# A share of the exps of an attention kernel moved from ScalarE to VectorE, and extra work emitted only where it is needed

## The chip, the cores and the metric

The kernel runs on one core of a Trainium2 chip. The metric is the device time of one execution in microseconds. Times are medians of several executions. Ratios are the mean time of one kernel's fast runs over the mean time of the other's fast runs of the same rounds, so they are not quite the ratio of the medians quoted. Chips and rounds differ a little: the kernel before took 2049 us beside the changed kernel and 2042 to 2045 us beside the experiments, so kernels of different rounds are compared by ratio.

## The reference, cut to what matters

```python
B, S, D, H, Dff = 1, 2048, 512, 32, 1792
x = x + attention(layernorm(x), wqkv, wo)      # 32 heads of 16
x = x + relu(layernorm(x) @ w1) @ w2
x = x + attention(layernorm(x), wqkv, wo)      # the same weights again
x = x + relu(layernorm(x) @ w1) @ w2
```

Two attention layers of 32 heads over 2048 rows need 2 x 32 x 2048 x 2048 exps. In the trace of the kernel before, the exps keep ScalarE busy for 1847.9 us, and all matmuls, repeats included, keep TensorE busy for 1690.9 us.

## The kernel before: the parts that matter

Queries are taken 512 at a time. A block is 128 keys by 512 queries of one head. Three blocks make a slot: three score matmuls write three banks of a score buffer (there are two buffers), one exp reads all 1536 columns, and two slots later the blocks are multiplied by the values into one output bank, `ps_o`. A segment is 16 key blocks by 4 heads, 64 blocks, some 21 slots; at its end VectorE copies `ps_o` out. (A few segments of the second layer are cut into two parts by keys: what the first part summed is stored, and loaded again with the second. The change leaves these alone.) Projections and the dense layers are worked off between the slots in small pieces, through one bank, `ps_f`.

```python
while blocks:                                   # one slot
    ...
    for sg, kb, g in now:                       # what this slot needs
        run_until(("q", sg["n"]))
        run_until(("k", sg["l"], sg["T"], kb // TPC))
    ...
    for _ in range(times):                      # 1 to 3: repeats up to FLOOR = 3.4 passes a slot
        for w, (sg, kb, g) in enumerate(now):
            ...
            nc.tensor.matmul(b[:, w, :], ...)   # scores
    ex = nc.scalar.activation(out=eb[:, :m, :], in_=b[:, :m, :], func=ACTF.Exp, scale=SCALE)
    ...
    run_evac()                                  # copies out of ps_f that are due
    ...
    while len(pend) > 1:
        emit_pv()                               # the slot before last times the values
    ...
    spent = run_pe(pace) if todo else 0.0       # other matmuls, in pieces
    ...
    run_dve(900)                                # other VectorE work

def force():                                    # used by run_until
    if evac:
        run_evac()
        return True
    if cur or pick(emitted):
        cur.popleft()[1]()
        return True
    ...
```

`run_until(key)` forces work: it writes down other work at once, until the wanted result is in the lists. All this decides only the order in which each engine's instructions are written down. Every engine then works off its own list in that order and waits at an instruction until what it needs is there.

The softmax here doesn't subtract the row's maximum and nothing guards it: scores larger than these inputs give would overflow.

## Time and profile before

| | before |
|---|---|
| time, median | 2049.5 us |
| profiled span | 2037.9 us |
| exps (three blocks each) | 1366, busy 1847.9 us |
| ScalarE idle before exps | 55.1 us |
| TensorE waiting for exps | 218.8 us |
| VectorE busy | 436.9 us (21%) |
| mean granted TensorE clock | 0.971 |

Idle time ahead of the exps is time that the bound engine loses. TensorE's wait for exps is its reserve. The lines themselves stand in the prediction.

### The profile page before, as it was taken

What the parts mean: (1) busy time and instruction counts of PE and PEld (TensorE: products, weight loads), DVE (VectorE), ACT (ScalarE), POOL (GpSimd) and SP (SyncE); (2) the same over time, 40 slices, a digit from 0 to 9 for tenths busy, and PEclk for the clock granted to TensorE, in tenths of its full rate; (3) what the DMA queues carried; (4) which work ended last, traced back from release to release, by engine and by line L of the source; (5) the groups of instructions that cost most, each with busy time, mean ns of one, the idle gap of its engine ahead of it and who ended that gap; (6) DMA issues with size and microseconds to landing.
All of it is one profiled execution on the core that took longest, in us unless ns stands there. A gap on an engine that the chain in (4) does not pass through costs nothing.

```text
span 2037.9 us, 30025 instructions
## 1 busy us (share of the span) xinstructions
PE 1690.9 (83%) x13604; PEld 523.4 (26%) x13604; DVE 436.9 (21%) x927; ACT 1871.7 (92%) x1407; POOL 2.4 (0%) x35
## 2 busy tenths in 40 slices
PE   5777778888888888888889877898888888888876
PEld 2222222222222222222222222222222222222222
DVE  5111102212132132212133220211112111121122
ACT  2799999999999999999989999999999999999960
POOL 0000000000000000000000000000000000000000
PEclk8999999999999999999899989989998999989998
DMA  4000000000000000000000010000000000000000
GB/s 155 1 12 12 12 7 12 12 12 6 12 12 11 7 12 12 10 8 12 12 1 1 4 30 9 9 12 12 17 12 12 10 12 19 12 9 10 17 11 11
DMA packets 34131, 29.42 MB, mean 14 GB/s; under 512 B 17492, under 2 KB 25428, under 8 KB 34004
## 3 DMA queue, kind: packets, MB, share of 16 engines
q1 hardware_dynamic: 32420, 25.94, 5.6%
q8 instruction: 106, 1.74, 0.3%
q10 hardware_dynamic: 1584, 1.57, 0.2%
q14 instruction: 21, 0.17, 0.0%
HBM read 7.86 MB, written 2.10 MB: 5 GB/s over the span
## 4 chain that ended last, share of the span: by engine, by line
ACT 71%; PE 17%; DVE 8%; DMA 3%; issue 1%; SPq 0%; DVEq 0%
ACT e L628 71%; PE ps_s L621 6%; PE ps_f L243 5%; PE ps_o L545 4%; DMA r<-u 2%; PE ps_s L243 2%; DVE u L494 1%; DVE ht L400 1%; DVE q L371 1%; PE ps_s L579 1%; DVE stats L260 1%; DMA u<-c 1%; PE ps_f L298 0%; DVE xn L288 0%; ACT xnT L573 0%
## 5 line engine op out<-in xcount | busy, mean ns | idle before, releaser
L628 ACT ACTIVATE e<-ps_s 128x1536 bf16<-128x1536 f32 x1366 | 1847.9, 1581 | 55.1 <-PE ps_s L621 54.2
L621 PE MATMUL ps_s<-q,ktp 32*128 32x512 bf16 x7704 | 812.2, 385 | 221.2 <-ACT e L628 218.8
L545 PE MATMUL ps_o<-e,vaug 128*32 128x512 bf16 x4096 | 568.7, 396 | 45.3 <-DVE u L494 34.6
L621 PEld LDWEIGHTS <-ktp 32*128 32x128 bf16 x7704 | 257.2, 92 | 714.5 <-issue 659.7
L545 PEld LDWEIGHTS <-vaug 128*32 128x32 bf16 x4096 | 138.1, 93 | 490.3 <-issue 490.3
L243 PE MATMUL ps_f<-xn2T,w 128*128 128x512 bf16 x400 | 121.2, 391 | 11.1 <-DVE q L371 5.1
L400 DVE TENSOR_SCALAR ht<-ps_f 128x512 bf16<-128x512 f32 x99 | 68.4, 691 | 281.0 <-PE ps_f L243 281.0
L243 PE MATMUL ps_f<-w,ht 128*128 128x512 bf16 x406 | 120.0, 383 | 1.0
L499 DVE SCALAR_TENSOR_TENSOR ot<-u,mask,r 128x512 bf16<-128x512 f32 (+1 forms) x67 | 48.7, 727 | 276.5 <-DMA r<-u 273.8
L494 DVE COPY u<-ps_o 128x512 f32<-128x512 f32 x58 | 40.1, 691 | 266.5 <-PE ps_o L545 266.5
L243 PE MATMUL ps_f<-xnT,wqkv 128*128 128x512 bf16 x248 | 74.1, 389 | 1.4 <-DVE vaug L363 0.2
L371 DVE TENSOR_SCALAR q<-ps_f,mask 128x512 bf16<-128x512 f32 x68 | 47.9, 746 | 90.2 <-PE ps_f L243 90.2
L243 PE MATMUL ps_f<-wo,ot 128*128 128x512 bf16 x224 | 66.2, 386 | 0.8
L414 DVE TENSOR_TENSOR x<-x,ps_f 128x512 bf16<-128x512 bf16 x29 | 20.0, 688 | 189.2 <-PE ps_f L243 189.2
L386 DVE TENSOR_TENSOR x<-x,ps_f 128x512 bf16<-128x512 bf16 x28 | 19.2, 687 | 161.1 <-PE ps_f L243 161.1
L243 PEld LDWEIGHTS <-w 128*128 128x128 bf16 x448 | 32.0, 99 | 76.4 <-issue 67.5
L260 DVE BATCH_NORM_STATS2 stats<-x 128x6 f32<-128x512 bf16 x64 | 44.0, 687 | 7.0 <-DMA x<-in_A_x_dram 5.6
L338 DVE CAST ktp<-ps_f 128x512 bf16<-128x512 f32 x28 | 19.4, 692 | 117.1 <-PE ps_f L243 117.1
L243 PEld LDWEIGHTS <-ht 128*128 128x128 bf16 x448 | 29.1, 97 | 57.5 <-issue 47.9
L398 ACT ACTIVATE ht<-ps_s 128x512 bf16<-128x512 f32 x6 | 3.6, 597 | 42.8 <-PE ps_s L243 42.8
L298 PE MATMUL ps_f<-ident,xn 128*128 128x128 bf16 x188 | 21.8, 249 | 16.3 <-DVE xn L288 10.0
L298 PEld LDWEIGHTS <-xn 128*128 128x128 bf16 x256 | 18.4, 109 | 54.6 <-DVE xn L288 31.7
(54 smaller groups left out, 303.1 us busy)
## 6 DMA issues: line engine op xcount, KB each, us to landing
r<-u SPq DMA_DIRECT2D x63, 256.0 KB
w<-in_B_w_dram SPq DMA_DIRECT2D x2, 1792.0 KB
x<-in_A_x_dram SPq DMA_DIRECT2D x16, 128.0 KB
out_dram<-x SPq DMA_DIRECT2D x16, 128.0 KB
wqkv<-in_A_wqkv_dram ACTq DMA_DIRECT2D x3, 512.0 KB
c<-u SPq DMA_DIRECT2D x63, 8.0 KB
u<-c SPq DMA_DIRECT2D x63, 8.0 KB
wo<-in_A_wo_dram SPq DMA_DIRECT2D x1, 512.0 KB
```

The costliest lines, as they stand in the source:

```text
L243: nc.tensor.matmul(b, lhsT, rhs, start=(i == 0), stop=(i == n - 1))
L260: nc.vector.bn_stats(out=st[:], in_=x_t[j * TPC + i][:])
L298: nc.tensor.transpose(pt[:, c * P : (c + 1) * P], xnbuf[i][:, c * P : (c + 1) * P], ident[:])
L371: nc.vector.tensor_scalar(out=qbuf[n % 2][e][:], in0=b, scalar1=mask[e][:, 0:1], scalar2=None, op0=ALU.mult,)
L400: nc.vector.tensor_scalar(out=ht[ft][:], in0=b, scalar1=0.0, scalar2=None, op0=ALU.max)
L414: nc.vector.tensor_add(out=x_t[tt][:], in0=x_t[tt][:], in1=b)
L494: nc.vector.tensor_copy(out=u[:], in_=ps_o[:])
L499: nc.vector.scalar_tensor_tensor(out=ot[t][:, a : a + w], in0=u[:, a : a + w], scalar=mask[e][:, 0:1], in1=r[:, a : a + w], op0=ALU.mult, ...
L545: nc.tensor.matmul(ps_o[32 * g : 32 * g + 32, :], vaug[sg["l"]][kb][:, 4 * sg["T"] + g, 2 * e : 2 * e + 32], s["e"][:, w, :], start=(kb == ...
L579: nc.tensor.matmul(b, lhsT, rhs, start=(i == 0), stop=(i == len(mms) - 1))
L621: nc.tensor.matmul(b[:, w, :], kt[32 * g : 32 * g + 32, kc : kc + P], qbuf[sg["n"] % 2][sg["e"]][32 * g : 32 * g + 32, :], start=True, sto ...
L628: ex = nc.scalar.activation(out=eb[:, :m, :], in_=b[:, :m, :], func=ACTF.Exp, scale=SCALE)
```

## The change

The intent: VectorE is idle for four fifths of the span, so it takes up to six blocks of a segment off ScalarE, in three pairs. A score, scaled so that one unit of log2 is 2^23, is turned into an integer, whose bits are the exponent and the mantissa of the exp; a quartic in the mantissa mends the value. A pair costs VectorE two first steps out of PSUM and five more steps over both blocks. Its result comes as a sum, so TensorE multiplies it by the values three times. The first step is declared free of ScalarE's read of the same buffer (it reads another bank). `run_until` now makes only what the wanted thing depends on.

```diff
+    PAIRS = ((0, 2), (6, 8), (12, 14))
+    BACKLOG = 5000.0
 ...
+    def finish_group():
+        while cur:
+            cur.popleft()[1]()
+        run_evac()
     def run_until(key):
-        while key not in made:
-            assert force(), key
+        if key in made:
+            return
+        finish_group()
+        if key in made:
+            return
+        t = maker[key]
+        for k in (*t["deps"], *t.get("after", ())):
+            run_until(k)
+        ...
 ...
+    def flush_pair():
+        run_until(pairs[0]["key"])
+        emit_pair()
+
+    def dve_block(half, sg, kb, g, src, ex, recent):
+        while half == 0 and pairs:
+            flush_pair()
+        first = nc.vector.tensor_scalar(
+            out=di[:, half, :].bitcast(I32), in0=src, scalar1=EXP_BIAS, scalar2=0.0,
+            op0=ALU.add, op1=ALU.max,
+        )
+        tc.declare_no_dep(
+            first.ins, ex.ins, reason="both only read the scores, and in different banks"
+        )
+        ...
+            steps = (
+                (690, lambda: bits(dm, 0x007FFFFF, 0x3E800000)),
+                (1260, lambda: step(dy, dm, C2, dm)),
+                (1260, lambda: step(dy, dy, C1, dm)),
+                (1260, lambda: step(de, dy, C0, di)),
+                (690, lambda: bits(di, 0x7F800000, KAPPA_BITS)),
+            )
+    def emit_pair():
+        ...
+        for rhs in (de, de, None):
+            for half, (kb, g) in halves:
+                pv(...)
 ...
+            if half == 0:
+                taken = load[0] + sum(t["cost"] for t in dve_q) < BACKLOG
+            if not taken:
+                half = None
+        m = len(now) - (half is not None)
 ...
-        run_dve(900)
+        run_dve(500.0)
```

There is one `di`, one `dm`, one `dy` and one `de`. So the next pair cannot begin before the one before has been multiplied: `dve_block` flushes it first, and the end of a segment does the same (cut above). This is called a forced end; a pair is open until it has been multiplied. `load` is the code's own model of VectorE's work in hand, in ns, and a pair is taken only while that and the queued tasks are under `BACKLOG`.

More of the change, by code (lines that the diff above doesn't have):

```diff
@@ L1 @@
+import math
 from contextlib import ExitStack
@@ L55 @@
     NACC = 6
+    LEAD, C2, C1, C0 = 0.43216083424908747, -0.036015386827967774, 0.769178243088122, 0.36146642138144963
+    KAPPA_BITS = 0x00170000
+    LOG2E = 1.4426950408889634
+    UNIT = float(1 << 23)
+    EXP_BIAS = (126.0 + math.log2(2.0 * LEAD)) * UNIT
+    PAIRS = ((0, 2), (6, 8), (12, 14))
     FLOOR = 3.4
+    BACKLOG = 5000.0
     ctx.enter_context(tc.manual_schedule())
@@ L66 @@
     mask = [sb([P, 1], FP32, f"mask{e}") for e in range(2)]
+    qmask = [sb([P, 1], FP32, f"qmask{e}") for e in range(2)]
     wqkv = sb([P, NDC, 3 * D], BF16, "wqkv")
@@ L89 @@
     ot = [sb([P, QS], BF16, f"ot{t}") for t in range(NT)]
-    acc = [sb([P, QS], FP32, f"acc{t}") for t in range(NACC)]
+    dm = sb([P, 2, QS], FP32, "dm")
+    dy = sb([P, 2, QS], FP32, "dy")
+    di = sb([P, 2, QS], FP32, "di")
+    de = sb([P, 2, QS], BF16, "de")
+    acc = [x[:, k, :] for x in (dm, dy, di) for k in range(2)]
     ebuf = [sb([P, W, QS], BF16, f"e{n}") for n in range(NE)]
@@ L148, in mark @@
         made[key] = slot[0] + lag
-    def emitted(deps):
-        return all(k in made for k in deps)
-    def ready(deps):
-        return all(k in made and (wide[0] or made[k] < slot[0]) for k in deps)
     cur = deque()
@@ L160, with task, group, ready @@
     dve_q = []
+    maker = {}
+    load = [0.0]
+    owed = [0.0]
+    def task(cost, fn, makes=(), deps=(), after=(), first=False):
+        t = {"cost": cost, "fn": fn, "makes": makes, "deps": deps, "after": after}
+        if first:
+            dve_q.insert(first - 1, t)
+        else:
+            dve_q.append(t)
+        maker.update({k: t for k in makes})
+    def group(pieces, makes, deps):
+        g = {"pieces": pieces, "makes": makes, "deps": deps}
+        maker.update({k: g for k in makes})
+        return g
+    def ready(t):
+        return all(k in made and (wide[0] or made[k] < slot[0]) for k in t["deps"]) and all(
+            k in made for k in t.get("after", ())
+        )
     def left():
@@ L165, in left, with start_group @@
         )
-    def pick(test):
-        for q in (urgent, work):
-            for g in q:
-                if test(g["deps"]):
-                    q.remove(g)
-                    cur.extend(g["pieces"])
-                    return True
-        return False
-    owed = [0.0]
+    def start_group(g):
+        (urgent if g in urgent else work).remove(g)
+        cur.extend(g["pieces"])
     def run_pe(budget):
@@ L182, in run_pe @@
             if not cur:
-                if evac or not pick(ready):
+                g = None if evac else next((g for q in (urgent, work) for g in q if ready(g)), None)
+                if g is None:
                     break
+                start_group(g)
             c, fn = cur.popleft()
@@ L189, in run_pe, with do_task, run_dve, mm_group @@
         return spent
-    def run_dve(budget):
-        i = 0
-        while i < len(dve_q) and budget > 0:
-            c, deps, fn = dve_q[i]
-            if ready(deps):
-                dve_q.pop(i)
-                fn()
-                budget -= c
-            else:
-                i += 1
+    def do_task(t):
+        dve_q.remove(t)
+        t["fn"]()
+        load[0] += t["cost"]
+        for k in t["makes"]:
+            if k not in made:
+                mark(k)
+    def run_dve(limit):
+        while load[0] < limit:
+            t = next((t for t in dve_q if ready(t)), None)
+            if t is None:
+                return
+            do_task(t)
     def run_evac():
         while evac:
-            evac.popleft()()
-    def force():
-        if evac:
-            run_evac()
-            return True
-        if cur or pick(emitted):
-            cur.popleft()[1]()
-            return True
-        for i, (c, deps, fn) in enumerate(dve_q):
-            if emitted(deps):
-                dve_q.pop(i)
-                fn()
-                return True
-        return False
-    def run_until(key):
-        while key not in made:
-            assert force(), key
-    def run_all():
-        while force():
-            pass
-        assert not (urgent or work or dve_q or cur)
-    def mm_group(mms, fin, deps, per=2):
+            c, fn = evac.popleft()
+            fn()
+            load[0] += c
+    def finish_group():
+        while cur:
+            cur.popleft()[1]()
+        run_evac()
+    def run_until(key):
+        if key in made:
+            return
+        finish_group()
+        if key in made:
+            return
+        t = maker[key]
+        for k in (*t["deps"], *t.get("after", ())):
+            run_until(k)
+        if "pieces" in t:
+            start_group(t)
+            finish_group()
+        else:
+            do_task(t)
+        assert key in made, key
+    def run_all():
+        while True:
+            finish_group()
+            g = next((g for q in (urgent, work) for g in q if ready(g)), None)
+            if g is not None:
+                start_group(g)
+            elif dve_q:
+                do_task(next(t for t in dve_q if ready(t)))
+            else:
+                break
+        assert not (urgent or work)
+    def mm_group(mms, fin, makes, deps, per=2, cost=690):
         hold = {}
@@ L244, in piece @@
                 if a + per >= n:
-                    evac.append(lambda: fin(b))
+                    evac.append((cost, lambda: fin(b)))
             pieces.append((min(per, n - a), piece))
-        return {"pieces": pieces, "deps": deps}
+        return group(pieces, makes, deps)
     ln_seq = []
@@ L308, in ln_rows @@
         prev = ln_seq[ln_seq.index(tag) - 1]
-        dve_q.append((750, [], lambda: ln_stats(tag, j, i)))
+        task(750, lambda: ln_stats(tag, j, i), [("st", tag, i)])
         if i == TPC - 1:
-            dve_q.append((2400, [], lambda: ln_rstd(tag)))
+            task(2400, lambda: ln_rstd(tag), [("rs", tag)], after=all4("st", tag))
             for k in range(TPC):
-                dve_q.append((420, [("xT", prev, k)], lambda k=k: ln_apply(tag, j, k)))
+                task(
+                    420, lambda k=k: ln_apply(tag, j, k), [("xn", tag, k)],
+                    [("xT", prev, k)], [("rs", tag)],
+                )
     def ln_groups(tag, dst, war):
@@ L324, in fin @@
                     mark(("xnT", tag, i))
-                evac.append(fin)
-            groups.append({"pieces": [(1.3, piece)], "deps": [("xn", tag, i)] + war})
+                evac.append((430, fin))
+            groups.append(
+                group([(1.3, piece)], [("xT", tag, i), ("xnT", tag, i)], [("xn", tag, i)] + war)
+            )
         return groups
@@ L341, in k_group @@
     def k_group(l, T, j):
-        return mm_group(k_mms(T, j), lambda b: k_fin(l, T, j, b), all4("xnT", ("ln1", l, j)))
+        return mm_group(
+            k_mms(T, j), lambda b: k_fin(l, T, j, b), [("k", l, T, j)],
+            all4("xnT", ("ln1", l, j)),
+        )
     def v_mms(kb):
@@ L364, in fin @@
             mark(("v", l, kb))
-        return mm_group(v_mms(kb), fin, all4("xnT", ("ln1", l, kb // TPC)))
+        return mm_group(v_mms(kb), fin, [("v", l, kb)], all4("xnT", ("ln1", l, kb // TPC)))
     def q_group(run, n, l, j, T):
@@ L371, in fin @@
                 nc.vector.tensor_scalar(
-                    out=qbuf[n % 2][e][:], in0=b, scalar1=mask[e][:, 0:1], scalar2=None,
+                    out=qbuf[n % 2][e][:], in0=b, scalar1=qmask[e][:, 0:1], scalar2=None,
                     op0=ALU.mult,
@@ L378, in q_group @@
             [(wqkv[:, c, T * P : (T + 1) * P], xnT[j][:, c, :]) for c in range(NDC)],
-            fin, all4("xnT", ("ln1", l, j)),
+            fin, [("q", n)], all4("xnT", ("ln1", l, j)), cost=1400,
         )
@@ L391, in o_group @@
             [(ot[t][:, i * P : (i + 1) * P], wo[:, t // 2, :]) for t in range(NT)], fin,
+            [("o", l, j, i)],
             [("ot", l, j, t, i) for t in range(NT)],
@@ L406, in h_group @@
             [(w1[:, c, ft * P : (ft + 1) * P], xn2T[:, c, :]) for c in range(NDC)], fin,
-            all4("xnT", ("ln2", l, j)) + war,
+            [("h", l, j, ft)], all4("xnT", ("ln2", l, j)) + war,
         )
@@ L422, in z_group @@
             [(ht[ft][:, i * P : (i + 1) * P], w2[:, ft, :]) for ft in range(NF)], fin,
+            [("z", l, j, i)],
             [("h", l, j, ft) for ft in range(NF)],
@@ L460, in add_run @@
                     "l": l, "j": j, "t": 2 * T + e, "e": e, "T": T, "kbs": kbs, "n": n,
-                    "load": load, "store": store,
+                    "load": load, "store": store, "begun": set(),
                 }
@@ L483, in finish_segment @@
         l, j, t, e = sg["l"], sg["j"], sg["t"], sg["e"]
+        load[0] += 690
         if sg["store"]:
-            nc.vector.tensor_copy(out=acc[t][:], in_=ps_o[:])
+            nc.vector.tensor_copy(out=acc[t], in_=ps_o[:])
             return
@@ L488, in finish_segment @@
         norm_no[0] += 1
+        if n > 1:
+            run_until(("m", n - 2))
         u, r, c = ubuf[n % 2], rbuf[n % 2], cbuf[n % 2]
@@ L491, in finish_segment @@
         if sg["load"]:
-            nc.vector.tensor_add(out=u[:], in0=acc[t][:], in1=ps_o[:])
+            nc.vector.tensor_add(out=u[:], in0=acc[t], in1=ps_o[:])
         else:
@@ L526, in recip @@
                 mark(("r", n), 4)
-            dve_q.append((250, [("c", n)], recip))
-            dve_q.append((700, [("r", n)] + war, lambda: mul(0, QS)))
+            task(250, recip, [("r", n)], [("c", n)])
+            task(
+                700, lambda: mul(0, QS), [("ot", l, j, t, i) for i in range(TPC)] + [("m", n)],
+                [("r", n)] + war,
+            )
         if t == NT - 1:
@@ L533, with pv @@
     pend = deque()
-    last_exp = [None] * NE
+    exps = [deque(maxlen=6) for _ in range(NE)]
+    def pv(sg, kb, g, rhs, stop=False):
+        e = sg["e"]
+        nc.tensor.matmul(
+            ps_o[32 * g : 32 * g + 32, :],
+            vaug[sg["l"]][kb][:, 4 * sg["T"] + g, 2 * e : 2 * e + 32],
+            rhs, start=g not in sg["begun"], stop=stop,
+            tile_position=(0, 32 * g), skip_group_check=True,
+        )
+        sg["begun"].add(g)
     def emit_pv():
@@ L543, in emit_pv @@
             sg, kb, g, w = s["blocks"].popleft()
-            e = sg["e"]
-            nc.tensor.matmul(
-                ps_o[32 * g : 32 * g + 32, :],
-                vaug[sg["l"]][kb][:, 4 * sg["T"] + g, 2 * e : 2 * e + 32],
-                s["e"][:, w, :],
-                start=(kb == sg["kbs"][0]), stop=(kb == sg["kbs"][-1]),
-                tile_position=(0, 32 * g), skip_group_check=True,
-            )
-            if kb == sg["kbs"][-1] and g == 3:
+            last = kb == sg["kbs"][-1]
+            if last:
+                while pairs and pairs[0]["sg"] is sg:
+                    flush_pair()
+            pv(sg, kb, g, s["e"][:, w, :], last)
+            if last and g == 3:
                 finish_segment(sg, sg is segs[-1])
@@ L555, in emit_pv, with bits, step @@
             pend.popleft()
+    pairs = deque()
+    pair_no = [0]
+    def flush_pair():
[3 more added lines that the diff above has]
+        while half == 0 and pairs:
+            flush_pair()
+        first = nc.vector.tensor_scalar(
+            out=di[:, half, :].bitcast(I32), in0=src, scalar1=EXP_BIAS, scalar2=0.0,
+            op0=ALU.add, op1=ALU.max,
+        )
+        tc.declare_no_dep(
+            first.ins, ex.ins, reason="both only read the scores, and in different banks"
+        )
+        for earlier in recent:
+            tc.declare_no_dep(
+                first.ins, earlier,
+                reason="the scores read here were written after it, and are waited for",
+            )
+        load[0] += 690
+        if half == 0:
+            pair_no[0] += 1
+            pairs.append({"sg": sg, "key": ("e", pair_no[0]), "blocks": []})
+        pairs[-1]["blocks"].append((kb, g))
+        if half == 1:
+            def bits(out, keep, put):
+                nc.vector.tensor_scalar(
+                    out=out[:].bitcast(I32), in0=di[:].bitcast(I32), scalar1=keep,
+                    scalar2=put, op0=ALU.bitwise_and, op1=ALU.bitwise_or,
+                )
+            def step(out, x, c, y):
+                nc.vector.scalar_tensor_tensor(
+                    out=out[:], in0=x[:], scalar=c, in1=y[:], op0=ALU.add, op1=ALU.mult
+                )
+            key = pairs[-1]["key"]
+            steps = (
[4 more added lines that the diff above has]
+                (690, lambda: bits(di, 0x7F800000, KAPPA_BITS)),
+            )
+            for n, (cost, fn) in enumerate(steps):
+                k = key + (n,) if n + 1 < len(steps) else key
+                task(cost, fn, [k], after=[key + (n - 1,)] if n else [], first=n + 1)
+    def emit_pair():
+        p = pairs.popleft()
+        halves = list(enumerate(p["blocks"]))
+        tops = di[:].bitcast(BF16)
+        for rhs in (de, de, None):
+            for half, (kb, g) in halves:
+                pv(p["sg"], kb, g, tops[:, half, 1::2] if rhs is None else rhs[:, half, :])
     for j in range(NQS):
@@ L568 @@
                     op=ALU.add, axis=mybir.AxisListType.XY,
+                )
+            for e in range(2):
+                nc.vector.tensor_scalar(
+                    out=qmask[e][:], in0=mask[e][:], scalar1=SCALE * LOG2E * UNIT, scalar2=None,
+                    op0=ALU.mult,
                 )
@@ L599 @@
     level = 0.0
+    taken = False
+    recents = [[], []]
     while blocks:
@@ L626 @@
                 )
-        m = len(now)
-        ex = nc.scalar.activation(out=eb[:, :m, :], in_=b[:, :m, :], func=ACTF.Exp, scale=SCALE)
-        if last_exp[no % NE] is not None:
+        sg, kb, g = now[-1]
+        r = (kb * 4 + g - 2) // W
+        half = None
+        if len(now) == W and now[0][0] is sg and not (sg["load"] or sg["store"]):
+            half = next((p.index(r) for p in PAIRS if r in p), None)
+            if half == 0:
+                taken = load[0] + sum(t["cost"] for t in dve_q) < BACKLOG
+            if not taken:
+                half = None
+        m = len(now) - (half is not None)
+        ex = nc.scalar.activation(
+            out=eb[:, :m, :], in_=b[:, :m, :], func=ACTF.Exp,
+            scale=1.0 / (LOG2E * UNIT),
+        )
+        for earlier in exps[no % NE]:
             tc.declare_no_dep(
-                ex.ins, last_exp[no % NE],
+                ex.ins, earlier,
                 reason="the matmuls that read the buffer between the two writes order them",
             )
-        last_exp[no % NE] = ex.ins
+        exps[no % NE].append(ex.ins)
+        recent = recents[no % 2]
+        recents[no % 2] = [ex.ins] + recent[:1]
+        load[0] = max(load[0] - 50.0 - 427.0 * m, 0.0)
         run_evac()
+        if half is not None:
+            dve_block(half, sg, kb, g, b[:, W - 1, :], ex, recent)
         for sg, kb, g in now:
@@ L639 @@
             emit_pv()
-        pend.append({"e": eb, "blocks": deque(x + (w,) for w, x in enumerate(now))})
+        if pairs and ready({"deps": [pairs[0]["key"]]}):
+            emit_pair()
+        pend.append({"e": eb, "blocks": deque(x + (w,) for w, x in enumerate(now[:m]))})
         rest = len(blocks) / W % per_chunk
@@ L644 @@
         spent = run_pe(pace) if todo else 0.0
+        sg = now[-1][0]
         level = min(level + times + 1 + spent - FLOOR, 0.4)
-        run_dve(900)
+        run_dve(500.0)
     while pend:
```

## The prediction

> **What bounds the kernel now.** I read the page from the top: busy shares, the chain that ended last, then the costliest groups, and after that the timeline of a quiet stretch and the waits by engine.
>
> ```profile
> PE 1690.9 (83%) x13604; PEld 523.4 (26%) x13604; DVE 436.9 (21%) x927; ACT 1871.7 (92%) x1407; POOL 2.4 (0%) x35
> ...
> ACT 71%; PE 17%; DVE 8%; DMA 3%; issue 1%; SPq 0%; DVEq 0%
> ACT e L628 71%; PE ps_s L621 6%; PE ps_f L243 5%; PE ps_o L545 4%; DMA r<-u 2%; PE ps_s L243 2%; DVE u L494 1%; DVE ht L400 1%; DVE q L371 1%; PE ps_s L579 1%; DVE stats L260 1%; DMA u<-c 1%; PE ps_f L298 0%; DVE xn L288 0%; ACT xnT L573 0%
> ...
> L628 ACT ACTIVATE e<-ps_s 128x1536 bf16<-128x1536 f32 x1366 | 1847.9, 1581 | 55.1 <-PE ps_s L621 54.2
> ```
>
> The reader is to see that ScalarE is busy 92% of the span, that the exps are 71% of the chain, and that the exp line is busy 1847.9 us with only 55.1 us of idle before it. The mean of 1581 ns counts overlap between neighbours; 1847.9 / 1366 = 1.353 us is what one exp of three blocks (1536 columns) costs the engine. The exps run from 67 us to 1970 us, a main stretch of some 1903 us; the roughly 67 us ahead of it and 68 us behind it are not touched by the change.
>
> The next question is how much room TensorE has, because the change gives it work too. One quiet stretch, start and duration first:
>
> ```profile
> 429.55 0.83 PE L621 MATMUL ps_s<-q,ktp 32*128 32x512 bf16 x9 [0.62 <-ACT e L628]
> ...
> 430.31 0.40 PE L545 MATMUL ps_o<-e,vaug 128*32 128x512 bf16 x3
> ...
> 430.63 0.61 PE L243 MATMUL ps_f<-w,ht 128*128 128x512 bf16 x2
> ...
> 431.17 0.39 PE L621 MATMUL ps_s<-q,ktp 32*128 32x512 bf16 x3
> ...
> 431.49 0.40 PE L545 MATMUL ps_o<-e,vaug 128*32 128x512 bf16 x3
> ...
> 431.82 0.60 PE L243 MATMUL ps_f<-w,ht 128*128 128x512 bf16 x2
> ...
> 432.36 0.39 PE L621 MATMUL ps_s<-q,ktp 32*128 32x512 bf16 x3
> ...
> 433.58 0.82 PE L621 MATMUL ps_s<-q,ktp 32*128 32x512 bf16 x9 [0.50 <-ACT e L628]
> ```
>
> Starts matter here, not durations. Three score matmuls occupy 0.32 us (431.17 to 431.49), nine 0.76 us (429.55 to 430.31), so each further pass of three costs (0.76 - 0.32) / 2 = 0.22 us and a change of kind some 0.1 us. The nine are one useful pass and two repeats, which the code's floor of 3.4 passes a slot (a slot is one exp) asks for. From 429.55 to 433.58 three slots pass, 1.343 us each, and TensorE stands still only about 0.5 to 0.6 us in them. Over the whole run the waits say the same:
>
> ```profile
> PE ps_s L621 <- ACT e L628: 218.8, 604, 0.8
> ...
> ACT e L628 <- PE ps_s L621: 54.2, 109, 2.4
> ...
> PE ps_o L545 <- DVE u L494: 34.6, 39, 2.3
> ```
>
> TensorE waits for ScalarE 218.8 us in all. That is its whole reserve: whatever shortens the exps and whatever is added to TensorE both come out of it. VectorE is free for four fifths of the span.
>
> **What the Trainium skill says.** "ScalarE: Activation LUTs", section What ACT_TABLE_LOAD costs: an ACTIVATE takes 186 ns + 0.833 ns a column, and neighbours overlap by about 93 ns. For 1536 columns that is 1.37 us; the trace has 1.35. So taking 512 columns off an exp should save 0.427 us, by 0.833 x 512. No run here yet shows an exp of 1024 columns.
> "VectorE: DVE Perf Modes", section on the perf-mode tier table: fp32 single-source operations within SBUF run at twice the rate, two-source ones and anything from PSUM in fp32 at one element a cycle. The trace agrees as far as it goes: copying 512 fp32 columns out of PSUM takes 691 ns, and the two-source scalar_tensor_tensor of 512 fp32 columns 751 ns.
> "PSUM — Partial Sum Buffer", Specifications: ScalarE and VectorE may read PSUM in parallel at full bandwidth as long as they are in different banks. The change relies on it (VectorE takes the third bank of a score buffer, ScalarE the first two). The trace of before has no such case.
> "TensorEngine Tiling (Array Packing)", Key Properties: different tiles run in parallel, and changing the tiling mode drains the engine. The 0.22 us for three matmuls and the 0.1 us at a change of kind agree with both.
>
> **The change part by part.** Off ScalarE: in each of 58 segments that are neither stored nor loaded (64 blocks, 21.3 slots) up to six slots, in three pairs, give their last block to VectorE. One pair saves 2 x 0.427 = 0.854 us of exps. All 58 x 3 = 174 pairs would save 148.6 us, 7.3%.
>
> On VectorE, one pair costs: two first steps out of PSUM at 0.69 (the 691 ns row) = 1.38; two bit operations over 1024 elements at double rate, 0.69 each (512 cycles' worth, like the row of 512) = 1.38; three scalar_tensor_tensor of 1024, which I put at 751 ns plus 512 further elements at 1/0.96 ns (533), less a little for immediate scalars, 1.26 each = 3.78. Together 6.54 us. 174 pairs would be 1138 us on top of 437, so over three quarters of the span; the five steps in a row behind the second first step are 5.16 us and, with small gaps, 5.5 us.
>
> How many pairs are taken? The code refuses a pair when its modelled load plus the queued tasks exceed 5000 ns. The pairs sit at slots 0 and 2, 6 and 8, 12 and 14. After slot 2 the model issues about one step a slot, and none in a slot with an evacuation (690). At slot 6, without an evacuation in between, load 1260 plus two steps left 1950 plus reciprocal and scaling of the segment before 950 make 4160: taken. With one evacuation, one step more is left: 5420, refused. Evacuations: from the rows of the groups some 279 in 1366 slots, 0.20 a slot, so no evacuation in three slots has a chance of 0.8^3 = 0.51; layer-norm tasks (4080 at once) refuse a few more, so the second pair is taken in about 0.43 of the segments. The first I put at 0.93. The third is taken in 0.9 of the cases where the second was refused and 0.45 where it was taken: 0.57 x 0.9 + 0.43 x 0.45 = 0.70. Sum 2.06 a segment, 120 pairs. They save 120 x 0.854 = 102 us on ScalarE and bring VectorE 120 x 6.54 = 785 us, to some 1220 us.
>
> On TensorE, a moved block is multiplied by the values three times instead of once. The two blocks of a pair are two column groups apart and run side by side, in the same mode as the matmuls before: three passes of 0.22 = 0.65 us a pair, 78 us in all. The repeats of the scores are not reduced by it, since the floor doesn't count these matmuls.
>
> Lost again: where a pair follows a taken one at four slots' distance (0.43 + 0.19 = 0.62 a segment, 36 in all), the rest of the chain is forced right behind the scores. From the end of the exp two slots before the pair's second slot: the chain ends after 0.35 + 0.75 + 5.5 = 6.6 us; the scores of slot 6 are done after 1.35 + 0.93 + 2 x 1.35 + 0.32 = 5.3 us. TensorE waits 1.3 us, then 0.65 us of pair, 0.65 us of other work, 0.35 us of scores: the next exp can start at 8.2 us, whereas ScalarE is through at 7.2. So 1.0 us of ScalarE idle, 36 us in all; such a pair gains nothing. Evacuations that queue behind a step of up to 1.26 us: about half of the 279 fall into slots with a chain, 0.3 us of TensorE lost each (42 us), of which I let a third reach the exps, 14 us. Forcing work only by need can take away some of the 54.2 us; 41 of those waits, 21.3 us, lie between 1000 and 1250 us, where stored and loaded segments force work. I take 8 us.
>
> Sum for ScalarE: -102 + 36 + 14 - 8 = -60 us. TensorE has to agree: of its reserve of 218.8 go 78 for the new matmuls, 36 x 1.3 = 47 for forced pairs and 42 for late evacuations, which leaves 52 us by which the span can shrink before TensorE is full. The two limits are close, so both engines would set the end together; I choose the tighter one and predict 2049.5 - 52 = 1998 us. That VectorE's first step doesn't wait for the exp of the same scores is already in this: I let it start as soon as the scores are there.
>
> **The rivals.** First: nearly all is hidden. If VectorE keeps up and most pairs are taken, 150 pairs save 128 us, the span goes to 1920 to 1950 us. For it: VectorE is idle 79% now and double buffering swallows nearly an exp. Against it: the chain of 5.5 us against four slots of 5 us, and TensorE, which would need 128 + 98 = 226 us of a reserve of 218.8.
> Second: TensorE becomes the bound. Its idle time goes to nothing, waits of ScalarE for scores grow from 54 us to 100 us or more, and the time stays at 2005 to 2035 us. For it: the reserve above. Against it: part of TensorE's work is repeats.
> Third: the new waits on VectorE (pair matmuls, score banks released late, evacuations late) cost more than the exps save, and a TensorE that stands still is granted a lower clock: the mean is 0.971 now. Then 2050 to 2090 us. For it: after a stall of 2.39 us at 1797 us the next six exps came 1.6 to 1.9 us apart instead of 1.35. Against it: the refusal rule keeps VectorE's queue short.
>
> **Range and chances.** The middle is 1998 us (2.5% less). The range 1950 to 2037 us covers most of the first and all of the second rival. The line of 2% is 2008.5 us, near the middle; faster by over 2% 0.63, within 2% 0.31, slower by over 2% 0.06.
>
> **What would show it.** Right: the exps' busy time falls to about 1745 us, some 240 of them with 1024 columns at about 0.93 us; VectorE busy around 1220 us, its two-source steps 1.26 us each; 480 more matmuls into the output bank (three for each of the 240 moved blocks instead of one); ScalarE's waits for scores rise to about 90 to 100 us, with new waits of TensorE on the pair's last bit step. Wrong: more than 150 or fewer than 90 pairs; the reserve of TensorE (its waits on exps) still over 120 us, which would mean that I overrated its work; steps at other durations; a mean granted clock away from 0.97.

## The result, and the profile after

The changed kernel takes 2104.95 us (2100.59 to 2106.41, 4 runs) against 2049.45 us: ratio 1.0268, 95% interval 1.0248 to 1.0287. It is slower by 2.7%, where 2.5% faster was predicted, and lies outside the range.

First the page's busy line, the chain that ended last by engine, and the exp line of the changed kernel (L772 is its exp, L756 its score matmul).

```profile
PE 1758.3 (84%) x13926; PEld 542.3 (26%) x14087; DVE 1155.7 (55%) x1734; ACT 1792.3 (85%) x1407; POOL 2.4 (0%) x35
...
ACT 52%; PE 32%; DVE 13%; issue 2%; DMA 1%; another core or an unknown queue 0%; SPq 0%; DVEq 0%; ACTq 0%
...
L772 ACT ACTIVATE e<-ps_s 128x1536 bf16<-128x1536 f32 (+1 forms) x1366 | 1768.4, 1410 | 199.2 <-PE ps_s L756 195.7
```

The exps did become cheaper: busy 1768.4 us instead of 1847.9, 79.5 us less. But ScalarE's idle time before them went from 55.1 to 199.2 us, 144.1 us more. The sum, +64.6 us, is the growth of the profiled span (2101.8 - 2037.9 = 63.9 us). ScalarE's share of the chain falls from 71% to 52%; TensorE and VectorE now stand in it with 32% and 13%.

Next the groups by form (count, busy time, mean ns of one).

```profile
L772 ACT ACTIVATE e<-ps_s 128x1536 bf16<-128x1536 f32 x1135 | 1563.3, 1482 | 162.6 <-PE ps_s L756 159.3
...
L635 DVE TENSOR_SCALAR di<-ps_s 128x512 int32<-128x512 f32 x230 | 158.8, 690 | 342.3 <-PE ps_s L756 306.1
...
L661 DVE SCALAR_TENSOR_TENSOR dy<-dm 128x1024 f32<-128x1024 f32 x115 | 140.7, 1224 | 3.2
...
L772 ACT ACTIVATE e<-ps_s 128x1024 bf16<-128x1024 f32 x230 | 243.5, 1059 | 36.6 <-PE ps_s L756 36.4
...
L655 DVE TENSOR_SCALAR di<-di 128x1024 int32<-128x1024 int32 x115 | 79.6, 692 | 3.3
```

115 pairs were taken (230 first steps), and the steps cost what had been worked out: 690, 1224 and 692 ns. The cost of the work is not where the prediction failed. The waits are (engine and line, whom it waited for, us in total, times, longest):

```profile
ACT e L772 <- PE ps_s L756: 195.7, 191, 6.3
PE ps_s L756 <- ACT e L772: 132.3, 393, 0.6
...
PE ps_o L598 <- DVE de L661: 51.2, 28, 3.9
```

Before, ScalarE's longest wait for scores was 2.4 us; now it is 6.3 us. TensorE still waits 132.3 us for exps, so it is not full. New is its wait for a step of the pair, 28 times, up to 3.9 us. The longest stall in order of time (start, duration; L423 copies a query projection out of `ps_f`, L598 multiplies by the values, L287 are the other matmuls):

```profile
681.67 0.39 PE L756 MATMUL ps_s<-q,ktp 32*128 32x512 bf16 x3
681.99 0.61 PE L287 MATMUL ps_f<-xnT,wqkv 128*128 128x512 bf16 x2
682.64 1.41 DVE L423 TENSOR_SCALAR q<-ps_f,qmask 128x512 bf16<-128x512 f32 x2 [1.54 <-PE ps_f L287]
683.96 1.22 DVE L661 SCALAR_TENSOR_TENSOR dy<-dy,dm 128x1024 f32<-128x1024 f32 x1
685.21 1.23 DVE L661 SCALAR_TENSOR_TENSOR de<-dy,di 128x1024 bf16<-128x1024 f32 x1
686.47 0.69 DVE L655 TENSOR_SCALAR di<-di 128x1024 int32<-128x1024 int32 x1
686.49 1.04 PE L598 MATMUL ps_o<-de,vaug 128*32 128x512 bf16 x4 [3.89 <-DVE de L661]
...
688.29 1.03 PE L287 MATMUL ps_f<-xn2T,w 128*128 128x512 bf16 x2
689.26 0.61 PE L756 MATMUL ps_s<-q,ktp 32*128 32x512 bf16 x3
...
689.91 1.45 ACT L772 ACTIVATE e<-ps_s 128x1536 bf16<-128x1536 f32 x1 [6.34 <-PE ps_s L756]
```

Read it downward. The slot's scores come at 681.67; then the current group of projection matmuls is finished (681.99) and VectorE has to copy it out, 1.41 us, and only then come the three steps of the open pair that were left, two of which the first pair matmuls need. TensorE stands for 3.89 us with the pair's matmuls at the head of its list. This is `flush_pair`: `run_until` calls `finish_group` before the wanted steps. VectorE was idle for 1.54 us just before, waiting for that group. After the wait TensorE is slow besides: two matmuls take 1.03 us that took 0.61 us at 681.99. Two stretches of 14 us (start and end, length, busy time of PE, PEld, DVE, ACT and POOL, then the granted clock, the DMA share and GB/s):

```profile
682.00:696.00 14.00, 9.32 (x42) 1.91 (x39) 7.13 (x9) 4.88 (x5) 0.00 (x0) 0.63 0.01 2
520.00:534.00 14.00, 11.77 (x116) 3.80 (x117) 9.18 (x12) 14.00 (x12) 0.00 (x0) 1.00 0.09 19
```

Around the stall the granted clock was 0.63, and ScalarE was busy 4.88 us of 14; in a stretch with a pair that was not forced it was 1.00, and ScalarE was busy throughout.

I put every stall of the exps down to the longest wait of TensorE between 1.5 us before the stall and its end (waits for exps left out). 35 stalls with 108 us follow a wait for a pair's steps; before the change all stalls together were some 55 us. The stall shown is the worst kind and not the only one: in 18 of the 35, matmuls of a group stand between the slot's scores and the pair's matmuls (70.0 us, 3.9 us a stall); in 17 none do (38.1 us, 2.2 us a stall). The theory, called F below: the forced ends of pairs cost the time. Rivals: T, TensorE is too full with added matmuls and repeats, and S, the new way of giving out work costs time of itself.

### The profile page after: what moved, and what is told of

The parts are those of the page before. It is cut to its first block, busy times and chain, and to the rows that moved or that the text cites. A ratio compares the mean times of both kernels' runs of the same rounds, so it can differ in the third digit from the quotient of the medians.

```text
span 2101.8 us, 31777 instructions
## 1 busy us (share of the span) xinstructions
PE 1758.3 (84%) x13926; PEld 542.3 (26%) x14087; DVE 1155.7 (55%) x1734; ACT 1792.3 (85%) x1407; POOL 2.4 (0%) x35
## 4 chain that ended last, share of the span: by engine, by line
ACT 52%; PE 32%; DVE 13%; issue 2%; DMA 1%; another core or an unknown queue 0%; SPq 0%; DVEq 0%; ACTq 0%
ACT e L772 51%; PE ps_s L756 11%; PE ps_f L287 9%; PE ps_o L598 9%; DVE de L661 2%; DVE dy L661 2%; DVE ht L453 2%; DVE u L551 1%; PE ps_s L287 1%; DVE q L423 1%; DVE di L655 1%; PE ps_s L712 1%; DVE ktp L387 1%; DVE vaug L415 1%; DVE x L467 0%
## 5 line engine op out<-in xcount | busy, mean ns | idle before, releaser
L772 ACT ACTIVATE e<-ps_s 128x1536 bf16<-128x1536 f32 (+1 forms) x1366 | 1768.4, 1410 | 199.2 <-PE ps_s L756 195.7
L756 PE MATMUL ps_s<-q,ktp 32*128 32x512 bf16 x7727 | 819.8, 388 | 145.2 <-ACT e L772 132.3
L598 PE MATMUL ps_o<-e,vaug 128*32 128x512 bf16 x3866 | 586.9, 399 | 42.9 <-DVE u L551 33.7
L756 PEld LDWEIGHTS <-ktp 32*128 32x128 bf16 x7727 | 241.9, 92 | 643.2 <-issue 574.9
L635 DVE TENSOR_SCALAR di<-ps_s 128x512 int32<-128x512 f32 x230 | 158.8, 690 | 342.3 <-PE ps_s L756 306.1
L598 PEld LDWEIGHTS <-vaug 128*32 128x32 bf16 x4556 | 168.6, 94 | 599.8 <-issue 579.5
L661 DVE SCALAR_TENSOR_TENSOR dy<-dm 128x1024 f32<-128x1024 f32 x115 | 140.7, 1224 | 3.2
L661 DVE SCALAR_TENSOR_TENSOR dy<-dy,dm 128x1024 f32<-128x1024 f32 x115 | 140.7, 1223 | 3.2
L661 DVE SCALAR_TENSOR_TENSOR de<-dy,di 128x1024 bf16<-128x1024 f32 x115 | 140.7, 1223 | 3.0
L598 PE MATMUL ps_o<-de,vaug 128*32 128x512 bf16 x460 | 81.1, 403 | 51.4 <-DVE de L661 51.2
L287 PE MATMUL ps_f<-xn2T,w 128*128 128x512 bf16 x358 | 111.7, 390 | 12.4 <-issue 3.3
L287 PE MATMUL ps_f<-w,ht 128*128 128x512 bf16 x361 | 107.6, 383 | 10.0 <-issue 5.6
L655 DVE TENSOR_SCALAR di<-di 128x1024 int32<-128x1024 int32 x115 | 79.6, 692 | 3.3
L655 DVE TENSOR_SCALAR dm<-di 128x1024 int32<-128x1024 int32 x115 | 79.5, 691 | 2.9
L287 PE MATMUL ps_f<-xnT,wqkv 128*128 128x512 bf16 x209 | 68.5, 402 | 8.5 <-issue 4.6
L423 DVE TENSOR_SCALAR q<-ps_f,qmask 128x512 bf16<-128x512 f32 x68 | 47.9, 746 | 37.7 <-PE ps_f L287 35.7
L287 PE MATMUL ps_f<-wo,ot 128*128 128x512 bf16 x196 | 59.8, 383 | 5.8 <-issue 2.9
L598 PE MATMUL ps_o<-di,vaug 128*32 128x512 bf16 x230 | 55.3, 415 | 7.6 <-DVE di L655 5.2
```

The source lines that it names most:

```text
L287: nc.tensor.matmul(b, lhsT, rhs, start=(i == 0), stop=(i == n - 1))
L423: nc.vector.tensor_scalar(out=qbuf[n % 2][e][:], in0=b, scalar1=qmask[e][:, 0:1], scalar2=None, op0=ALU.mult,)
L598: nc.tensor.matmul(ps_o[32 * g : 32 * g + 32, :], vaug[sg["l"]][kb][:, 4 * sg["T"] + g, 2 * e : 2 * e + 32], rhs, start=g not in sg["begun ...
L635: first = nc.vector.tensor_scalar(out=di[:, half, :].bitcast(I32), in0=src, scalar1=EXP_BIAS, scalar2=0.0, op0=ALU.add, op1=ALU.max,)
L655: nc.vector.tensor_scalar(out=out[:].bitcast(I32), in0=di[:].bitcast(I32), scalar1=keep, scalar2=put, op0=ALU.bitwise_and, op1=ALU.bitwise_or,
L661: nc.vector.scalar_tensor_tensor(out=out[:], in0=x[:], scalar=c, in1=y[:], op0=ALU.add, op1=ALU.mult)
```

## The experiments

**No pairs.** The list of pairs is emptied; the new giving out of work stays.

```diff
-    PAIRS = ((0, 2), (6, 8), (12, 14))
+    PAIRS = ()
```

> The list of pairs is empty: no block goes to VectorE, everything else of the change stays (work forced by need, load model, shared buffers). Theory F (the loss of 55 us is the forced ends of pairs): about the time of before, 2035 to 2055 us, exps waiting some 50 us for scores. Rival S (the new way of giving out work costs time by itself): 2080 us or more, waits of the exps well over 100 us without any pair. Rival T (TensorE is full because of the added matmuls): also as before.

Measured 2035.98 us beside 2045.45 us, ratio 0.9958 (0.9920 to 0.9996), exps waiting 46.3 us for scores. S falls: this part of the change costs nothing and gains about 9 us (1 to 16 us by the interval).

**No forced end from the next pair.** A pair is refused while the one before is open.

```diff
-                taken = load[0] + sum(t["cost"] for t in dve_q) < BACKLOG
+                taken = load[0] + sum(t["cost"] for t in dve_q) < BACKLOG and not pairs
```

> A pair is refused while the pair before it is unfinished, so no pair's end is forced by the next one. Theory F: the stalls over 1 us that follow a wait of TensorE for a pair's steps (34 of them, about 108 us in the changed kernel) go, pairs fall from 115 to about 95 or so, time 1985 to 2020 us. Rival T (TensorE full, or VectorE in the way of evacuations): the stalls move elsewhere, time 2060 us or more.

Measured 1995.71 us beside 2045.45 us, ratio 0.9761 (0.9733 to 0.9788), with 97 pairs. One condition turns 2.7% slower into 2.4% faster. The waits of this kernel:

```profile
ACT e L772 <- PE ps_s L756: 78.8, 125, 5.0
...
PE ps_s L756 <- ACT e L772: 139.3, 421, 0.7
...
PE ps_o L598 <- DVE de L661: 5.9, 3, 2.6
```

TensorE's waits for `de` went from 28 to 3 (with those for the pair's last step, from 35 to 6), and the waits of the exps from 195.7 to 78.8 us. They did not move elsewhere. F holds here; as the pairs also became fewer, the next run keeps more of them.

**Two pairs, nine slots apart.** Forcing is made rarer by distance, at nearly the same number of pairs.

```diff
-    PAIRS = ((0, 2), (6, 8), (12, 14))
+    PAIRS = ((0, 2), (11, 13))
```

> Two pairs a segment, nine slots apart instead of four (three pairs before). Theory F: about 105 to 112 pairs, nearly as many as now, hardly any of them forced, exps busy about 1770 us, waits of the exps 60 to 110 us, time 1980 to 2015 us. Rival T: TensorE gets nearly the same added work (about 108 pairs), so the time stays at 2070 us or more.

Measured 2015.00 us (2013.71 to 2021.94), ratio 0.9868 (0.9834 to 0.9902), with 108 pairs, exps busy 1772.9 us and waiting 104.1 us for scores. That is the upper edge of what F allowed and far from T. Distance doesn't end forcing: seven stalls with 15.5 us still follow a wait for a pair's steps. It is slower than the run before with more pairs. TensorE waits up to 3.8 us for the copy at a segment's end here (39.0 us in all), where it was 0.8 us (31.1 us). I take it that the later pair's chain runs into that end; no run tests this.

**One multiplication instead of three.** The result is wrong (relative error 0.073).

```diff
-        for rhs in (de, de, None):
+        for rhs in (None,):
```

> A moved block is multiplied once instead of three times (the result is wrong on purpose); the pairs, the steps and the forcing stay. Theory F: TensorE's added matmuls are not the cause: 10 to 30 us less than the changed kernel, still over 2065 us. Rival T: the added matmuls are the cause, 75 us less or more, under 2030 us.

Measured 2149.95 us, ratio 1.0515 (1.0458 to 1.0572), at a mean granted clock of 0.919: slower than the changed kernel, with less work. Neither theory had expected that. 34 stalls with 111 us follow a wait for a pair's step, about as before; the other stalls grew from 91 to 129 us. It is against T, but it needed the run below.

**The same without forcing.**

```diff
-                taken = load[0] + sum(t["cost"] for t in dve_q) < BACKLOG
+                taken = load[0] + sum(t["cost"] for t in dve_q) < BACKLOG and not pairs
 ...
-        for rhs in (de, de, None):
+        for rhs in (None,):
```

> A moved block multiplied once (wrong result on purpose) and no pair forced. It tells why one_pass became slower, 45 us over the changed kernel, with less work. If the lack of matmuls alone lowers the granted clock: mean clock under 0.96 and a time over 2005 us. If it takes the forced stalls to lower it: clock about 0.98 and 1970 to 2000 us, not over no_force.

Measured 1989.56 us, ratio 0.9759 (0.9721 to 0.9796), clock 0.980 (result wrong). The ratio is that of no_force, 0.9761. So the two added multiplications cost nothing that these runs show (the intervals are 0.3 to 0.4% wide to either side) where the next pair forces nothing: T falls. Fewer matmuls alone didn't lower the clock; together with the forced stalls they did. Why the two together do so is not settled here.

**The forced end kept, but the pair's steps alone.** The pairs and their places are those of the changed kernel; the current group is no longer put in front.

```diff
     def flush_pair():
-        run_until(pairs[0]["key"])
+        key = pairs[0]["key"]
+        while key not in made:
+            do_task(dve_q[0])
         emit_pair()
```

> The changed kernel with the forced end kept (same pairs, same places) but only the pair's open VectorE steps are forced: TensorE's current group and its evacuation are no longer finished in front of them. If the loss per forced pair (3.2 us in the trace, where I had worked out 1.0) comes from the group and evacuation put in front: stalls of about 1.0 to 1.5 us each, time 2020 to 2050 us. If it comes from the chain of steps itself: 2085 us or more.

Measured 2025.84 us (2024.61 to 2026.19), ratio 0.9917 (0.9899 to 0.9935), with 114 pairs. From 1.0268 this is 3.5%, some 72 us, by the order of a few instructions. 23 stalls with 34.1 us are left behind a pair's step, 1.5 us each, none with a group in front, where it was 35 with 108 us, 3.1 us each. So about two thirds of the forced loss went with the group and its copy in front of the steps. It is what the whole edit is worth: it shifts later slots too, stalls that had no group in front among them, and 7530 score matmuls remain of 7727 (by the floor runs below I estimate these at some 4 us). At the place shown above, this kernel does this:

```profile
683.16 0.61 PE L598 MATMUL ps_o<-de,vaug 128*32 128x512 bf16 x4 [1.59 <-DVE de L663]
...
684.68 1.46 PE L758 MATMUL ps_s<-q,ktp 32*128 32x512 bf16 x9
...
686.19 1.45 ACT L774 ACTIVATE e<-ps_s 128x1536 bf16<-128x1536 f32 x1 [3.14 <-PE ps_s L758]
```

A wait of 1.59 us still becomes a stall of 3.14 us here, in part because nine score matmuls (two of the three passes are repeats) then take 1.46 us instead of 0.82.

**VectorE waits for the exp of the same scores.** no_force with the declaration taken out.

```diff
-        tc.declare_no_dep(
-            first.ins, ex.ins, reason="both only read the scores, and in different banks"
-        )
```

> As no_force (pair refused while one is open), but VectorE's first step waits for ScalarE's read of the same scores, as it would without the declaration of the change. If that wait matters: the first step comes after the exp, some 1 us later, the score buffer is released 0.7 us after the exp and the exps wait for scores at the 194 moved blocks; 20 to 80 us more than no_force, 2015 to 2075 us. If it is hidden by double buffering: 1995 to 2005 us.

Measured 2076.08 us (2063.20 to 2078.71), ratio 1.0147 (1.0105 to 1.0188), against 0.9761 for no_force: some 79 us. The waits of this kernel:

```profile
DVE di L635 <- ACT e L769: 524.1, 194, 10.4
...
ACT e L769 <- PE ps_s L753: 139.7, 227, 5.0
```

Each of the 194 first steps now waits for an exp, and VectorE's list stands behind it; TensorE in its turn waits 47.4 us for the first steps to free a score buffer. So that part of the change was needed, and double buffering does not hide it.

**No forced end, and the steps alone at a segment's end.** Both edits above together.

> no_force with the forcing that is left at segment ends (three stalls after a wait for a step, 12.0 us in no_force's trace) done by steps alone. Theory: 5 to 12 us less than no_force, 1983 to 1991 us.

Measured 1982.42 us (1982.06 to 1991.29) beside 2042.54 us, ratio 0.9716 (0.9690 to 0.9742), results correct. It is the fastest version measured, 2.8% faster than the kernel before; its interval just overlaps that of no_force, so what the second edit adds is less sure.

**Fewer repeats.** no_force with a floor of 2.8 instead of 3.4.

```diff
-    FLOOR = 3.4
+    FLOOR = 2.8
```

> no_force with a floor of 2.8 passes a slot instead of 3.4, so fewer repeats of the score matmuls. If TensorE's fullness holds the rest of the gain back: 10 us less or more than no_force, under 1986 us. If the repeats keep its clock up (as the one_pass run suggests, slower at a granted clock of 0.919): a lower granted clock and a longer time, over 2000 us.

Measured 2003.14 us (1989.84 to 2014.86), ratio 0.9805 (0.9752 to 0.9858), clock 0.938, at 5978 recorded score matmuls instead of 7650. The clock fell as the second view said; the time scatters too much to say more than that it is no gain.

**More repeats.** The best version with a floor of 3.8.

```diff
-    FLOOR = 3.4
+    FLOOR = 3.8
```

> no_force_steps_first with a floor of 3.8 passes a slot instead of 3.4: more repeats of the scores. If the clock is still what small stalls come from: clock above 0.982 and up to 10 us less. If TensorE is full enough by now: 10 to 60 us more, 1992 to 2045 us.

Measured 1998.56 us (1996.25 to 1999.04), ratio 0.9785 (0.9761 to 0.9809), clock 0.985. So more repeats cost 14 us or so: TensorE is not the bound, but its reserve is not free either.

**Pairs further apart and a longer backlog, twice.** The best version with

```diff
-    PAIRS = ((0, 2), (6, 8), (12, 14))
-    BACKLOG = 5000.0
+    PAIRS = ((0, 2), (7, 9), (13, 15))
+    BACKLOG = 7000.0
```

> no_force_steps_first with the pairs five slots apart instead of four ((0,2), (7,9), (13,15)) and a backlog limit of 7000 instead of 5000, so that the pair before is more often finished in time: 110 to 135 pairs instead of 97. Theory: each further pair is worth about 0.6 us (no_pairs to no_force_steps_first: some 54 us by 97 pairs), so 10 to 25 us less, 1958 to 1975 us. Rival (VectorE delays evacuations and the copy at the segment's end): 1980 us or more.

Measured 1994.75 us, ratio 0.9767 (0.9739 to 0.9796), with 89 pairs, not the 110 to 135 expected. My edit was careless: its second gap is still four slots, not five as I wrote. With (14, 16) as the third pair:

```diff
-    PAIRS = ((0, 2), (7, 9), (13, 15))
+    PAIRS = ((0, 2), (7, 9), (14, 16))
```

> As spaced_backlog with the third pair one slot later, so that both gaps are five slots: in spaced_backlog the second gap was still four, and only 89 pairs were taken. If the gap is what refuses pairs: 105 to 140 pairs, time 1965 to 1985 us. If late evacuations and copies eat the further pairs: more pairs, but 1985 us or more.

Measured 2006.91 us, ratio 0.9818 (0.9787 to 0.9848), with 86 pairs. Both outcomes expected were wrong: the gap is not what keeps the count down. Six waits for a pair's step, 9.9 us, are back. The traces show where the pairs went: counting the short exps by their slot, first pairs of a segment fell from 43 in no_force_steps_first to 32 and 29, second pairs rose from 15 to 26 and 29, third pairs fell from 39 to 31 and 28. A replay of the kernel's Python with the chip's calls left out, which gives the same counts, shows the reason of each refusal: in these two runs an open pair every time, never the backlog alone. A pair moved later is still open where the next one, often the first of the next segment, would begin.

## Why the prediction was wrong

The step that failed is "So 1.0 us of ScalarE idle, 36 us in all". Measured are 35 stalls behind a pair's step with 108 us, 3.1 us each. That their number came out was in part luck: the 36 were pairs that begin four slots after a taken one, and only 24 of the 35 stalls are there; 8 come where the first pair of a segment ends the last of the segment before, 2 at a segment's end and one at a distance of ten slots. The working let TensorE wait only for the chain of steps, already under way on VectorE. What it overlooked is in the diff: `flush_pair` goes through `run_until`, which finishes TensorE's current group and its copy out of `ps_f` before the steps. I had read `finish_group` as part of "forcing work only by need", which was to gain, and not asked what it puts in front of a forced pair. The 18 stalls with a group in front took 3.9 us each, behind waits of 2.0 us; steps_first, which takes the group away, gains 72 us. A second thing is missing in the 1.0 us: in the 17 stalls without a group TensorE waited 1.25 us on average, as worked out (1.3), and the exps still lost 2.2 us each; in steps_first it is 1.5 us. So the way from the wait to the next exp was put too short. In the stall shown of steps_first, the scores after the wait ran at about half speed and carried two repeats, 1.46 us where the working had 0.35; how much of the rest this explains was not tested.

Point by point:

- **ScalarE's saving.** Predicted 102 us by 120 pairs; measured 79.5 us by 115. The duration of a shorter exp was right (1.02 us alone against 1.45, a difference of 0.43). Five pairs fewer are 4 us. At 1.353 us for a full exp and 0.926 us for a short one, 1135 and 230 exps would take some 1749 us, and they took 1768.4. I put these 19 us down to exps that after a stall have no neighbour to overlap with (285 exps have idle time before them, 126 before the change; one alone takes 1.45 us instead of 1.353); no run tests this.
- **Forced pairs.** Predicted 36 us, measured 108 us. This is 72 of the 125 us between the predicted change of ScalarE's sum (-60) and the measured (+65).
- **Other stalls.** Predicted +14 - 8 = +6 us; measured 199 - 108 = 91 us against 55 before in the same reckoning, +36; some 16 us of it stand behind the copy at a segment's end. The 8 us for forcing by need were right (9 us in no_pairs).
- **TensorE's reserve.** Predicted to be all but used up, and the tighter limit. Wrong: TensorE still waits 132 us for exps, and one_pass_no_force shows the added multiplications to cost nothing. The second rival, TensorE as the bound, falls with it.
- **The third rival.** New waits on VectorE and a lower clock (0.960 instead of 0.971): of the three this is the one that happened, even beyond its 2050 to 2090 us, and I gave slower by over 2% a chance of 0.06. The refusal rule, my argument against it, bounds the queue in the model of the load; it doesn't bound what a forced flush puts into it.
- **VectorE's work and the wait removed.** Durations and busy time were right to some 5% (1155.7 us against some 1220). That the first step starts as soon as the scores are there was taken for granted; wait_exp shows it to be worth some 79 us.

With the forcing gone, no_force and the best version come to 0.9761 and 0.9716 of the time before; the predicted ratio was 0.975, though at fewer pairs (97). So the size of the gain was about right for a kernel that doesn't force; as the prediction had forced pairs and more pairs in it, that is in part chance.

## What to carry to other kernels

When work moves to an idle engine, ask what happens if it is not done in time, and read the code of that path line by line: a rare forced wait (35 in 1366 slots) took more (108 us) than all the saved work (79.5 us). If the moved piece can be refused, refuse it rather than wait for it; and if it must be waited for, put only the wanted steps in front, on the engine that has them.

## What the Trainium skill lacked or had wrong

- "TensorE: Matmul & The Clock Gate", section The HAM clock gate, puts the fall to half the clock after an idle window of about 3.4 us. In the steps_first run a single wait of 1.59 us, ended at 683.16, was followed by nine score matmuls in 1.46 us instead of 0.82; the granted clock was 1.00 from 680.7 to 684.1 and 0.50 from 684.1 to 687.5. The page says that the window runs freely, and elsewhere that frequent short idle times make the clock swing; it has no figure for how short a wait can be enough.
- No page has that fewer matmuls and stalls together lower the mean clock more than either: 0.919 (one_pass), 0.980 without the stalls, 0.960 with the stalls and all matmuls. No page gives the cost of a repeat kept for the clock either: a floor of 3.8 instead of 3.4 cost 14 us or so.
- "VectorE: DVE Perf Modes", section on the perf-mode tier table, has no row for scalar_tensor_tensor, and no page has a duration for it. Over 1024 fp32 elements with an immediate scalar it took 1223 ns, as this page's formula for a two-source fp32 add, in its section on the TRN2 errata, gives (1224).
- "ScalarE: Activation LUTs" was right: exps of 1024 and 1536 columns that stood alone took 1.02 and 1.45 us, where 186 ns + 0.833 ns a column gives 1.04 and 1.47. "PSUM — Partial Sum Buffer" was right as well: VectorE's read beside ScalarE's, in another bank, took 690 ns, like the 691 ns of a copy in the kernel before, and the shorter exp beside it 1.02 us.
